# A new opening for a kernel of windowed attention followed by an expanding layer with SoLU and LayerNorm

## The chip, the cores and the metric

The kernel runs on one core of a Trainium2 chip. The metric is device time in microseconds (us) for one execution, and lower is better. The core has five engines that run side by side, each with its own queue of instructions taken in order: TensorE (PE in the profile, with its weight loads as PEld), VectorE (DVE), ScalarE (ACT), GpSimd (POOL) and SyncE (SP). In this kernel all transfers between HBM and the core's memory are issued from SP's queue. PE writes its results to PSUM, which has eight banks of 512 fp32 columns; DVE and ACT read PSUM and SBUF, POOL works on SBUF alone.

## The reference

Eight batches of eight heads, 576 positions, 64 columns a head. The first four heads attend to the last 32 positions, the other four to every fourth of the last 128. What comes out is laid side by side as 4608 tokens of 512 values, and goes through a layer with a softmax gate and a normalisation:

```python
scores = np.where(mask, (q @ k.T) / np.sqrt(64), -1e9)
attn = softmax(scores);  x = attn @ v            # 4608 tokens x 512
h = x @ w_in                                     # 512 -> 1024
solu = h * softmax(h)
ln = (solu - mean(solu)) / np.sqrt(var(solu) + 1e-6) * g_ln
out = ln @ w_out                                 # 1024 -> 512
```

The data are fp32, and so is the accuracy wanted. The two weight matrices arrive as 64-bit floats, so the kernel itself has to turn them into fp32.

## The kernel before

**Products in three passes.** A product of two fp32 matrices is made with PE's faster fp32r type: each operand is split into a high part (the value rounded to fp32r) and a low part (the rest), and hi x hi, hi x lo and lo x hi are added up in PSUM. So `w_i` and `w_o` are kept as pairs, x as `x_hi` and `x_lo`, and the normalised tile t, turned, as `th` and `tl`.

**Weights.** They come in 16 blocks of 128 x 512 values (512 KB as 64-bit words): blocks 0 to 7 make `w_in` (block b holds rows b // 2 and column half b % 2), blocks 8 to 15 `w_out`. Of each block ACT makes `low` (the lower bits) and `abs` (the magnitude), DVE does `sign`, `clamp` and `join`, which put the fp32 words together; for blocks 8 to 15 ACT multiplies with `gain` (g_ln); ACT's `hi` rounds, and `lo` subtracts the rounded from the full value. Blocks 0 to 5 make `lo` on PE: `diff` (two matmuls, with the identity and with its negative `minus`) leaves the difference in a bank of 5 to 7, and ACT copies it out. From block 6 on POOL subtracts. Raw blocks land in slots that the middle layer uses later (t0 to t3, raw4, raw5).

**Attention, in units.** A unit is two heads of one batch, 32 in all; four units make the x of one batch, 4.5 tiles of tokens. For unit n: load `q` (kt, 312 KB, and qt, 296 KB) and `v` (384 KB); `S` (80 small matmuls, L220); `mask`, `max`, `sub`, `exp`, `sum`, `inv`, `norm`, `turn` (32 x 32 blocks transposed on DVE); `V` (up to 96 small matmuls, L294); `xh` (ACT) and `xl` (DVE) write high and low part of x. In units 0 to 3 the mask is put into the bank by PE and `sub` is DVE's; from unit 4 on `mask` is DVE's and `sub` POOL's. `norm` is DVE's throughout. V writes to the front columns of banks 4 to 7.

**Tiles of 128 tokens.** For each of 36 tiles i: `ha`, `hb`, `hc`, `hd` (24 matmuls of 128 x 512 together, L328) give h in two banks; `peak` (DVE), `e` (ACT), `gate` (DVE), `mid` (centring, on ACT for the tiles in ACT_CENTRE, else on DVE), `var` (a square with its sum on ACT, then a chain of six tiny operations on POOL that end in rstd). Then t has to be turned, features to the partitions. Tiles 0 to 5 and the last do it on PE: `t` (eight transposes, L399) into banks 3 and 4, `th` (ACT) and `tl` (DVE) out of them. All others take a detour over HBM: `forth` (four DMAs, L426) writes t, `back` (one DMA, L433) fetches it with its blocks exchanged, `tr0` and `tr1` transpose inside 32 x 32 blocks on DVE (L442), `th0`, `th1` (ACT, L450) and `tl0`, `tl1` (POOL, L455) split it. `o` (24 matmuls, L464) and `out` (ACT, and a DMA) end the tile.

**What sets the order.** The order of every instruction on every engine is written out in lists of words, a word for each step and its number; each engine follows its part of the list. INIT lists the first loads, all ahead of any other work; OPENING goes from the first conversion to tile 5 and unit 9, with o0 to o4 in it. From i = FIRST = 6 on, STEP is repeated for each tile: h of tile i, attention of the units that are due, and `o` of tile k. A tile that goes over HBM needs time, so in the steady state k = i - 2; tiles 0 to 5 have k one step behind, and step 7 (NO_SECOND_STEP) has no `o` at all, since there the lag goes from one step to two. A DMA stands in SP's queue at its place in the list, and SP waits there until its data and its slot are ready.

## Time and profile before

| what | value |
|---|---|
| median of 3 runs | 537.34 us (536.75 to 538.61) |
| the profiled execution | 538.63 us, its span 536.7 us |
| mean granted clock of PE | 0.975 |
| PE busy | 500.6 us (93%) |
| DVE, ACT, POOL busy | 355.6 (66%), 240.3 (45%), 186.8 us (35%) |
| chain that ended last | PE 85%, DVE 5%, DMA 5%, ACT 2%, issue 2% |

The span goes from the first to the last instruction. "Busy" is the time in which an engine has an instruction at work. Rows of groups give line, engine, operation, output and input with their shapes, the count, then busy time in all and the mean of one in ns, then idle time before them with what released it. Rows of waits give who waits, for whom, then the total, the number of waits and the longest. Rows of a timeline give start, length, engine, line and operation. The chain of waits follows back from the last instruction what released each step. The granted clock is the share of full speed that PE was allowed.

### The profile page before, as it was taken

The page shows a single profiled execution, that of the slowest core. Times are in us where ns is not written, and L with a number is a line of the kernel's source. Part 1 is how long each engine was busy: PE and PEld are TensorE (multiplying, and loading weights), DVE is VectorE, ACT ScalarE, POOL GpSimd, SP SyncE. Part 2 cuts the span into 40 slices and gives each one's busy share as a digit, 9 for nine tenths or more (in the row PEclk, how much of TensorE's full clock was granted, in tenths as well). Part 3 has the DMA queues.
Part 4 walks back from the last instruction along what each step waited for, and adds up shares of the span by engine and source line. Part 5 has one row for each costly group of instructions (what it writes and reads, how often), then busy time and mean ns, then how long its engine had stood idle before and what let it go on. Part 6 is the DMA issues. An engine that isn't in the chain of part 4 may idle for free.

```text
span 536.7 us, 16433 instructions
## 1 busy us (share of the span) xinstructions
PE 500.6 (93%) x7186; PEld 398.8 (74%) x7186; DVE 355.6 (66%) x554; ACT 240.3 (45%) x384; POOL 186.8 (35%) x316
## 2 busy tenths in 40 slices
...
GB/s 303 400 329 153 168 0 92 94 137 52 111 164 123 251 177 176 128 145 193 175 174 177 175 175 176 153 146 196 175 176 129 100 100 100 107 127 102 100 97 59
DMA packets 42983, 82.07 MB, mean 153 GB/s; under 512 B 5024, under 2 KB 20256, under 8 KB 42912
## 3 DMA queue, kind: packets, MB, share of 16 engines
...
q14 instruction: 15, 0.12, 0.1%
...
## 4 chain that ended last, share of the span: by engine, by line
PE 85%; DVE 5%; DMA 5%; ACT 2%; issue 2%; SPq 0%; ACTq 0%; DVEq 0%
PE banks L328 36%; PE banks L464 36%; PE banks L294 6%; PE banks L220 5%; DMA raw<-w_in 2%; PE banks L399 1%; DVE t L353 1%; DMA kt<-kT 1%; DMA t<-w_in 1%; PE banks L538 1%; DVE x_lo L315 1%; DVE nmax L339 1%; ACT x_hi L312 1%; DMA raw<-mid 1%; DVE mag L521 0%
## 5 line engine op out<-in xcount | busy, mean ns | idle before, releaser
L328 PE MATMUL banks<-w_i,x_hi 128*128 128x512 f32 x576 | 186.7, 405 | 5.9 <-DVE mu L353 5.7
L464 PE MATMUL banks<-w_o,th 128*128 128x512 f32 x576 | 180.8, 395 | 0.0
L328 PEld LDWEIGHTS banks<-w_i,x_hi 128*128 128x128 f32 x576 | 108.3, 193 | 32.0 <-DVE mu L353 6.2
L464 PEld LDWEIGHTS banks<-w_o,th 128*128 128x128 f32 x576 | 106.0, 188 | 21.6
L328 PE MATMUL banks<-w_i,x_lo 128*128 128x512 f32 x288 | 114.6, 398 | 0.0
L464 PE MATMUL banks<-w_o,tl 128*128 128x512 f32 x288 | 112.3, 390 | 0.0
L339 DVE TENSOR_REDUCE nmax<-banks 128x1 f32<-128x1024 f32 x36 | 44.0, 1221 | 65.3 <-PE banks L328 65.3
L455 POOL TENSOR_TENSOR tl<-t,th 128x512 fp32r<-128x512 f32 x58 | 74.2, 1302 | 32.1 <-ACT th L450 32.1
L259 ACT ACTIVATE sm<-sm 128x640 f32<-128x640 f32 x32 | 23.6, 737 | 97.6 <-POOL sm L255 97.6
L328 PEld LDWEIGHTS banks<-w_i,x_lo 128*128 128x128 f32 x288 | 55.3, 192 | 12.3
L464 PEld LDWEIGHTS banks<-w_o,tl 128*128 128x128 f32 x288 | 54.1, 188 | 11.7
L346 ACT ACTIVATE e<-banks,nmax 128x1024 f32<-128x1024 f32 x36 | 40.2, 1116 | 50.0 <-DVE nmax L339 47.3
L374 ACT ACTIVATE e<-t 128x1024 f32<-128x1024 f32 x29 | 30.8, 1062 | 53.5 <-DVE t L369 53.5
L234 DVE TENSOR_TENSOR sm<-banks,mask_sb 128x640 f32<-128x640 f32 x28 | 23.0, 822 | 46.7 <-PE banks L220 46.4
L353 DVE CUSTOM_DVE_ANT_0 t<-banks,e 128x1024 f32<-128x1024 f32 x36 | 43.8, 1216 | 15.2 <-ACT e L346 15.1
L255 POOL TENSOR_TENSOR sm<-sm,mx 128x640 f32<-128x640 f32 x28 | 35.3, 1262 | 47.0 <-DVE mx L246 41.6
L294 PEld LDWEIGHTS banks<-pt,vt 32*64 32x64 f32 x2816 | 34.6, 134 | 19.4 <-issue 10.6
L379 POOL TENSOR_SCALAR sq<-sq 128x1 f32<-128x1 f32 x36 | 11.0, 305 | 98.5 <-ACT e L374 98.2
L294 PE MATMUL banks<-pt,vt 32*64 32x64 f32 (+3 forms) x2816 | 38.5, 230 | 7.2 <-ACT w_i L545 3.6
L220 PEld LDWEIGHTS banks<-kt,qt 64*32 64x32 f32 x2560 | 29.4, 110 | 18.1 <-issue 14.4
L220 PE MATMUL banks<-kt,qt 64*32 64x64 f32 x2560 | 35.2, 235 | 5.8 <-issue 4.6
L450 ACT CAST th<-t 128x512 fp32r<-128x512 f32 x58 | 34.5, 619 | 11.4 <-DVE t L442 11.4
...
## 6 DMA issues: line engine op xcount, KB each, us to landing
...
```

The lines of the kernel that those rows point to most:

```text
L220: nc.tensor.matmul(out=ps[WIN * c : WIN * c + WIN, h, WQ * i : WQ * i + WQ], lhsT=qt[D * h : D * h + D, q0 : q0 + WIN], rhs=kt[D * h : D * ...
L255: eng.tensor_tensor(out=st[n]["sm"], in0=st[n]["sm"], in1=wide(mx), op=ALU.subtract)
L259: nc.scalar.activation(out=sm, in_=sm, func=AF.Exp, scale=0.125)
L294: nc.tensor.matmul(out=ps_x[D * h : D * h + D, c, c0 : c0 + k1 - k0], lhsT=vt[WIN * c : WIN * c + WIN, i, D * h : D * h + D], rhs=pt[WIN * ...
L328: nc.tensor.matmul(out=ps_h(i)[:, half], lhsT=a[:, kt, xs], rhs=w_i[:, kt, half, part, :], start=(kt == 0 and k == 0), stop=(kt == KT - 1 ...
L339: nc.vector.tensor_reduce(out=nmax, in_=h, axis=AX.X, op=ALU.max, negate=True)
L346: nc.scalar.activation(out=e, in_=h, func=AF.Exp, bias=nmax, scale=1.0, accum_out=se)
L353: nc.vector.tensor_tensor_reduce(out=t, in0=h, in1=ms[i]["e"], scale=1.0, scalar=0.0, op0=ALU.mult, op1=ALU.add, accum_out=mu,)
L374: nc.scalar.activation(out=e, in_=t, func=AF.Square, accum_out=sq)
L450: nc.scalar.copy(out=ms[i]["th"][:, cut(c)], in_=turned(i)[:, cut(c)])
L455: nc.gpsimd.tensor_tensor(out=ms[i]["tl"][:, cut(c)], in0=turned(i)[:, cut(c)], in1=ms[i]["th"][:, cut(c)].bitcast(F32), op=ALU.subtract,)
L464: nc.tensor.matmul(out=ps_o(i), lhsT=a[:, f, :], rhs=w_o[:, f, part, :], start=(f == 0 and k == 0), stop=(f == FT - 1 and k == 2),)
```

## The change

- **t over HBM from tile 0.** `by_dma` holds for all tiles but the last, so `t`, `th`, `tl` by way of PE are left for tile 35 alone. The lag is two steps from the start: k = i - 2, NO_SECOND_STEP is gone. The halves of the turn are called A and B, and in the opening they may come in either order.
- **Low parts.** `diff` with its matmuls, its copies on ACT and the tile `minus` are gone; `lo` is subtracted on POOL for twelve blocks and on DVE for blocks 2, 6, 13 and 15.
- **Clamps** of all blocks but 3, 5 and 6 go from DVE to POOL.
- **Normalising** of units 0 to 7 goes from DVE to POOL.
- **Centring** of tile 3 goes to DVE, that of tile 5 to ACT.
- **Order.** INIT and OPENING become one new list for all engines, loads among it. w1 is loaded first. The list reaches o3 (before: o4), and a word of STEP that the list holds already is skipped. 
- **Places.** h of tiles 0 and 2 is in banks 0 and 1, that of all others in banks 2 and 3; `o` alternates between banks 0 and 1 from tile 0; scores use banks 2 and 3 up to unit 4 (before: up to unit 9). Raw blocks have seven slots (SLOTS), with tp. The pad in front of `th0` is 24 values rather than 32.
- **A first Exp** on a column of constants (`ready`) stands ahead of everything on ACT.

The diff, with the old list cut:

```diff
--- before.py
+++ after.py
@@ -37,63 +37,54 @@
 SIGN_BIT = -(1 << 31)
 PE_MASK = (0, 1, 2, 3)
 POOL_SUB = True
-POOL_NORM = ()
-ACT_CENTRE = (0, 1, 2, 3)
+POOL_NORM = (0, 1, 2, 3, 4, 5, 6, 7)
+POOL_CLAMP = (0, 1, 2, 4, 7, 8, 9, 10, 11, 12, 13, 14, 15)
+DVE_LOW = (2, 6, 13, 15)
+ACT_CENTRE = (0, 1, 2, 5)
 Q_BUFS, V_BUFS, T_BUFS, TH_BUFS, CONV_BUFS = 4, 4, 4, 2, 4
 REBIAS = 2.0**16
 F64_MIN = REBIAS * float(np.array(0x38000000, np.uint32).view(np.float32))
 F64_MAX = REBIAS * float(np.array(0x47EFFFFF, np.uint32).view(np.float32))
-LOW_DIFF = 'mmmmmmpppppppppp'
 FIRST = 6
-INIT = "w0 q0 ib m0 i w1 v0 q1 w2 w3 v1 m1 q2 w4 w5 v2 g q3 v3"
 OPENING = (
-    "low0 abs0 sign0 clamp0 join0 w6 S0 q4 hi0 neg0 max0 low1 sub0 abs1 "
...
+    "w1 m0 low1 ib abs1 sign1 q0 clamp1 join1 S0 hi1 w0 max0 abs0 low0 q1 sub0 sign0 exp0 w3 "
+    "low3 clamp0 join0 sum0 w2 abs2 m1 lo1 inv0 S1 abs3 max1 q2 low2 sub1 S2 norm0 w5 w4 sign3 "
+    "clamp2 w7 turn0 v0 sign2 hi0 clamp3 low4 q3 w6 join3 low5 hi3 exp1 max2 V0 sub2 q4 sign4 "
+    "sign5 abs5 exp2 lo0 sum1 w9 lo3 v1 S3 inv1 join2 low7 sum2 v3 norm1 xh0 inv2 clamp5 abs4 "
+    "max3 xl0 turn1 sub3 g norm2 hi2 v2 clamp4 S4 w8 abs7 lo2 low6 w10 q5 join4 q7 V1 clamp7 "
+    "join5 abs6 v4 sign6 hi5 clamp6 exp3 q6 join6 xh1 hi6 sign7 sum3 lo5 inv3 low10 norm3 xl1 "
+    "low9 turn2 join7 mask4 w11 sign9 V2 abs9 hi4 ha1 xh2 clamp9 low8 lo4 max4 xl2 hi7 turn3 "
+    "ha0 sub4 abs8 exp4 sign10 w13 V3 lo6 v5 abs10 join9 lo7 sum4 inv4 xh3 abs11 xl3 w12 low11 "
+    "hc0 clamp10 clamp8 hb0 gain9 w14 join10 sign8 hd0 join8 norm4 S5 peak0 mask5 clamp11 low14 "
+    "max5 hi9 gain8 hc1 hd1 lo9 v6 turn4 V4 hi8 e0 gain10 sub5 hi10 low12 gate0 sign11 join11 "
+    "ha2 xh4 low13 xl4 lo8 exp5 lo10 mid0 abs12 S6 sum5 inv5 q8 hb1 norm5 hb2 clamp12 mask6 "
+    "max6 var0 peak1 gain11 sign14 e1 sub6 abs13 turn5 q9 hc2 forth0 abs14 hd2 gate1 back0 mid1 "
+    "sign13 peak2 hi11 clamp14 sign12 V5 clamp13 xh5 var1 xl5 exp6 forth1 join12 w15 join14 "
+    "gain12 gain14 join13 sum6 lo11 S7 hi12 ha3 inv6 mask7 e2 max7 norm6 v7 hc3 hi14 gain13 "
+    "abs15 sub7 trB0 turn6 V6 low15 back1 hd3 trB1 lo14 exp7 trA0 sign15 clamp15 thA0 gate2 xh6 "
+    "lo12 hi13 thB0 q10 tlA0 hb3 xl6 mid2 sum7 lo13 join15 S8 forth2 inv7 q11 gain15 hi15 tlB0 "
+    "mask8 norm7 back2 var2 peak3 lo15 e3 turn7 gate3 mid3 o0 max8 thB1 v8 V7 xh7 xl7 q12 ha4 "
+    "var3 trA1 thA1 tlA1 out0 sub8 hc4 exp8 trB2 forth3 trA2 hd4 tlB1 S9 hb4 peak4 v9 sum8 e4 "
+    "gate4 back3 thB2 mid4 trB3 thA2 o1 ha5 inv8 tlB2 hb5 tlA2 mask9 forth4 var4 hc5 norm8 "
+    "turn8 back4 hd5 o2 V8 v10 out1 v11 max9 trA3 thB3 trA4 peak5 trB4 thA3 sub9 e5 xh8 exp9 "
+    "xl8 thA4 out2 gate5 tlA3 tlB3 mid5 forth5 back5 thB4 sum9 inv9 o3 norm9 tlB4 var5 v12 "
+    "turn9 tlA4 out3 q13 i "
 )
 STEP = (
-    "back.j tr0.k th0.k tr1.k th1.k tl0.k tl1.k ha.i hb.i S.n q.n mask.n max.n sub.n hc.i hd.i "
+    "back.j trA.k thA.k trB.k thB.k tlA.k tlB.k ha.i hb.i S.n q.n mask.n max.n sub.n hc.i hd.i "
     "V.m v.m peak.i exp.n sum.n inv.n e.i gate.i mid.i forth.i xh.m xl.m var.i norm.n turn.n "
     "o.k t.i th.i tl.i out.k"
 )
-NO_SECOND = FIRST + 1
-NO_SECOND_STEP = (
-    "back.j ha.i hb.i S.n q.n mask.n max.n sub.n tr0.j tr1.j hc.i hd.i V.m v.m peak.i exp.n "
-    "xh.m sum.n xl.m e.i inv.n gate.i th0.j th1.j tl0.j tl1.j mid.i forth.i var.i norm.n turn.n"
+LAST_STEP = (
+    "back.j trA.k thA.k trB.k thB.k tlA.k tlB.k ha.i hb.i hc.i hd.i peak.i e.i trA.j trB.j "
+    "thA.j thB.j tlA.j tlB.j gate.i mid.i var.i o.k t.i th.i tl.i out.k"
 )
-LAST_STEP = (
-    "back.j tr0.k th0.k tr1.k th1.k tl0.k tl1.k ha.i hb.i hc.i hd.i peak.i e.i tr0.j tr1.j "
-    "th0.j th1.j tl0.j tl1.j gate.i mid.i var.i o.k t.i th.i tl.i out.k"
-)
-TURN = "tr0 th0 tr1 th1 tl0 tl1".split()
-BY_DMA = ["forth", "back", *TURN]
+BY_DMA = "forth back trA thA trB thB tlA tlB".split()
 BY_PE = "t.i th.i tl.i".split()
 LAST = NTILE - 1
-MERGED = 10
-SHIFT = {"th0": 32}
+SLOTS = "t0 t1 t2 t3 raw4 raw5 tp t0 t1 t2 t3 raw4 raw5 tp t3 tp".split()
+MERGED = 5
+SHIFT = {"th0": 24}
 
 
 @with_exitstack
@@ -130,7 +121,6 @@
     )
 
     id_sb = const.tile([P, P], F32, name="id_sb")
-    minus = const.tile([P, P], F32R, name="minus")
     mask_sb = const.tile([P, 2, NS * WQ], BF16, name="mask_sb")
     g_sb = const.tile([P, FT], F32, name="g_sb")
     id_bf = const.tile([P, P], BF16, name="id_bf")
@@ -145,10 +135,10 @@
     ps_t = (banks[:, 3, :], banks[:, 4, :])
 
     def ps_h(i):
-        return banks[:, 0:2] if i <= FIRST + 1 else banks[:, 2:4]
+        return banks[:, 0:2] if i in (0, 2) else banks[:, 2:4]
 
     def ps_o(i):
-        return banks[:, 2] if i < FIRST else banks[:, i % 2]
+        return banks[:, i % 2]
 
     def ps_s(n):
         if n < MERGED:
@@ -157,6 +147,8 @@
 
     nc.vector.memset(mhalf, -0.5)
     nc.vector.memset(below, -0.5 + 2.0**-14)
+    ready = const.tile([P, 1], F32, name="ready")
+    nc.scalar.activation(out=ready, in_=mhalf, func=AF.Exp)
 
     loaded = {}
 
@@ -185,14 +177,9 @@
 
     words = {}
 
-    def raw_slot(b):
-
-        k = b % 6 if b < 12 else b - 10
-        return f"t{k}" if k < T_BUFS else f"raw{k}"
-
     def load_w(b):
 
-        words[b] = moe.tile([P, 1024], F32, name=raw_slot(b), bufs=1).bitcast(I32)
+        words[b] = moe.tile([P, 1024], F32, name=SLOTS[b], bufs=1).bitcast(I32)
         w, row, col = (w_in, P * (b // 2), 512 * (b % 2)) if b < 8 else (w_out, P * (b - 8), 0)
         nc.sync.dma_start(
             out=words[b], in_=w.bitcast(I32)[row : row + P, 2 * col : 2 * (col + 512)]
@@ -417,7 +404,7 @@
             )
 
     def by_dma(i):
-        return FIRST <= i < LAST
+        return i < LAST
 
     def move_out(i):
 
@@ -445,12 +432,12 @@
         )
 
     def high_t(i, c):
-        if c == 0:
+        if "th" not in ms[i]:
             ms[i]["th"] = part_of_t("th", i)
         nc.scalar.copy(out=ms[i]["th"][:, cut(c)], in_=turned(i)[:, cut(c)])
 
     def low_t(i, c):
-        if c == 0:
+        if "tl" not in ms[i]:
             ms[i]["tl"] = part_of_t("tl", i)
         nc.gpsimd.tensor_tensor(
             out=ms[i]["tl"][:, cut(c)], in0=turned(i)[:, cut(c)],
@@ -503,7 +490,8 @@
 
     def conv_clamp(b):
 
-        nc.vector.tensor_scalar(
+        eng = nc.gpsimd if b in POOL_CLAMP else nc.vector
+        eng.tensor_scalar(
             out=cv[b]["mag"], in0=cv[b]["mag"], scalar1=F64_MIN, scalar2=F64_MAX,
             op0=ALU.max, op1=ALU.min,
         )
@@ -528,30 +516,13 @@
         nc.scalar.activation(out=cv[b]["mag"], in_=cv[b]["mag"], func=AF.Copy, scale=gain(b))
 
     def conv_hi(b):
-        if b < 8 or LOW_DIFF[b] == "p":
-            nc.scalar.copy(out=hi(b), in_=cv[b]["mag"])
-        else:
-            nc.scalar.activation(out=hi(b), in_=cv[b]["mag"], func=AF.Copy, scale=gain(b))
-
-    def conv_diff(b):
-        ps = cv[b]["ps"] = banks[:, 5 + b % 3, :]
-        nc.tensor.matmul(out=ps, lhsT=id_sb, rhs=cv[b]["mag"], start=True, stop=False)
-        nc.tensor.matmul(out=ps, lhsT=minus, rhs=hi(b), start=False, stop=True)
+        nc.scalar.copy(out=hi(b), in_=cv[b]["mag"])
 
     def conv_lo(b):
-        lo = w_part(b)[:, 1, :]
-        kind = LOW_DIFF[b]
-        if kind == "m":
-            nc.scalar.copy(out=lo, in_=cv[b]["ps"])
-        elif kind == "p":
-            nc.gpsimd.tensor_tensor(
-                out=lo, in0=cv[b]["mag"], in1=hi(b).bitcast(F32), op=ALU.subtract
-            )
-        else:
-            nc.vector.scalar_tensor_tensor(
-                out=lo, in0=cv[b]["mag"], scalar=1.0 if b < 8 else gain(b),
-                in1=hi(b).bitcast(F32), op0=ALU.mult, op1=ALU.subtract,
-            )
+        eng = nc.vector if b in DVE_LOW else nc.gpsimd
+        eng.tensor_tensor(
+            out=w_part(b)[:, 1, :], in0=cv[b]["mag"], in1=hi(b).bitcast(F32), op=ALU.subtract
+        )
         del cv[b]
 
     one = {
@@ -560,9 +531,8 @@
         "ib": lambda _: nc.sync.dma_start(out=id_bf, in_=ident_bf),
         "g": lambda _: nc.sync.dma_start(out=g_sb, in_=g_ln),
         "m": lambda d: nc.sync.dma_start(out=mask_sb[:, d], in_=mask[:, d]),
-        "neg": lambda _: nc.scalar.mul(out=minus, in_=id_sb, mul=-1.0),
         "abs": conv_abs, "low": conv_low, "clamp": conv_clamp, "sign": conv_sign,
-        "join": conv_join, "gain": conv_gain, "hi": conv_hi, "diff": conv_diff, "lo": conv_lo,
+        "join": conv_join, "gain": conv_gain, "hi": conv_hi, "lo": conv_lo,
         "S": scores, "mask": soft_mask, "max": soft_max, "sub": soft_sub, "exp": soft_exp,
         "sum": soft_sum, "inv": soft_inv, "norm": soft_norm, "turn": turn,
         "V": attend, "xh": spread_hi, "xl": spread_lo,
@@ -570,9 +540,9 @@
         "hc": lambda i: moe_h(i, 1, (0, 1)), "hd": lambda i: moe_h(i, 1, (2, 3)),
         "peak": moe_peak, "e": moe_exp, "gate": moe_gate, "mid": moe_centre, "var": moe_var,
         "forth": move_out, "back": move_back,
-        "tr0": lambda i: turn_t(i, 0), "tr1": lambda i: turn_t(i, 1),
-        "th0": lambda i: high_t(i, 0), "th1": lambda i: high_t(i, 1),
-        "tl0": lambda i: low_t(i, 0), "tl1": lambda i: low_t(i, 1),
+        "trA": lambda i: turn_t(i, 0), "trB": lambda i: turn_t(i, 1),
+        "thA": lambda i: high_t(i, 0), "thB": lambda i: high_t(i, 1),
+        "tlA": lambda i: low_t(i, 0), "tlB": lambda i: low_t(i, 1),
         "t": moe_t, "th": moe_th, "tl": moe_tl, "o": moe_o, "out": moe_out,
     }
     fronts = {}
@@ -580,27 +550,24 @@
         for r in range(NPAIR):
             fronts[(9 * b) // 2 - NPAIR - 1 + r] = NPAIR * b + r
 
-    for word in (INIT + " " + "".join(OPENING)).split():
+    for word in OPENING.split():
         name = word.rstrip("0123456789")
         one[name](int(word[len(name) :] or 0))
+    done = set(OPENING.split())
     for i in range(FIRST, NTILE + 2):
-        of = {
-            "n": fronts.get(i), "m": fronts.get(i - 1), "i": i, "j": i - 1,
-            "k": {FIRST: FIRST - 1, FIRST + 1: None}.get(i, i - 2),
-        }
-        words_of = {NO_SECOND: NO_SECOND_STEP, LAST: LAST_STEP}.get(i, STEP)
+        of = {"n": fronts.get(i), "m": fronts.get(i - 1), "i": i, "j": i - 1, "k": i - 2}
+        words_of = {LAST: LAST_STEP}.get(i, STEP)
         for word in (words_of if i <= LAST else "o.k out.k").split():
             name, which = word.split(".")
             n = of[which]
             if n is None or which in "ijk" and n >= NTILE:
                 continue
-            if i == NO_SECOND + 1 and name in TURN and which == "k":
-                continue
             if name in BY_DMA and not by_dma(n) or word in BY_PE and by_dma(n):
                 continue
             if name in "qv":
                 n += Q_BUFS if name == "q" else V_BUFS
-            one[name](n)
+            if f"{name}{n}" not in done:
+                one[name](n)
     assert not ms and not cv
 
 
```

25 rows, old and new, of the table OPENING are left out of this document.

## The prediction

> **What bounds the kernel now.** I read the clock and the span first, then the busy time by stage, then what TensorE (PE) waits for, and only then single rows. The stages, cut where the first output product o0 begins and where the opening list ends (columns: stretch, its length, busy time of each engine, granted clock, DMA share, GB/s):
>
> ```profile
> 0.00:81.12 81.12, 51.29 (x947) 35.86 (x947) 59.13 (x100) 52.57 (x86) 19.78 (x28) 0.83 0.63 224
> 81.12:140.60 59.48, 58.74 (x995) 47.55 (x994) 41.08 (x66) 25.67 (x41) 11.75 (x27) 1.00 0.32 95
> 140.60:536.70 396.10, 390.55 (x5251) 315.42 (x5249) 255.39 (x390) 162.09 (x259) 155.25 (x262) 1.00 0.49 147
> ```
>
> From 81.12 on PE is busy 449.3 of 455.6 us at clock 1.00: PE alone sets the pace, and an engine beside it buys nothing there. Before 81.12 it is busy 51.3 us, at clock 0.83. The waits of PE over the whole span say the same:
>
> ```profile
> PE banks L212 <- DMA mask_sb<-mask: 7.4, 1, 7.4
> PE banks L328 <- DVE mu L353: 5.7, 2, 4.7
> PE banks L220 <- issue: 4.6, 2, 3.1
> PE banks L294 <- ACT w_i L545: 3.6, 2, 3.2
> PE banks L294 <- DVE pt L278: 0.7, 1, 0.7
> PE banks L294 <- DVE sm L234: 0.4, 1, 0.4
> ```
>
> The first four lie in the opening; the last two are the 1.1 us at 169, where the old list changes its lag. So the change can pay only up to the point where PE is saturated, plus PE work that it removes. What PE's work costs when nothing is late, from the chain of waits (start, length, what), and the same work early on:
>
> ```profile
> 59.66 4.61 PE banks L328 x12
> ...
> 130.31 0.97 PE banks L220 x64
> ...
> 139.97 0.87 PE banks L399 x8
> ...
> 210.54 1.01 PE banks L294 x70
> ...
> 217.21 5.44 PE banks L328 x24
> ...
> 471.40 5.44 PE banks L464 x24
> ```
>
> By 81.12 PE has done h0 to h2 (16.3), S0 to S5 (5.8) and V0 to V3 (4.0): 26 us of lasting work in 81 us. The 55 us between are the prize.
>
> **Who is late in the opening.** VectorE (DVE) is busy 59 of those 81 us, ScalarE (ACT) 53, GpSimd (POOL) 20. Two later stretches of the opening:
>
> ```profile
> 43.00:59.70 16.70, 10.11 (x262) 6.77 (x260) 15.18 (x24) 13.16 (x22) 6.22 (x5) 0.90 0.64 201
> 59.70:81.12 21.42, 16.75 (x65) 13.30 (x65) 15.88 (x25) 16.39 (x28) 13.37 (x20) 0.76 0.11 38
> ```
>
> DVE instructions overlap in the records: the sum below begins at 12.00 and the next at 12.73, though the row says 0.81. I take 0.08 off each. Then DVE works 15.18 - 24 x 0.08 = 13.3 of 16.7 us (79%) in the first stretch and 13.9 of 21.4 (65%) in the second.
>
> **The end of the sum.** The new list reaches o0 later in its own order: before it stand S0 to S8, V0 to V6 and h0 to h3. What PE has left after o0's end is the old rest less what now lies earlier or is gone: 536.70 - 81.12 = 455.6, less o0 5.4, h3 5.4, S6 to S8 2.9, V4 to V6 3.0, four of the t transposes on PE (t2 to t5) 3.5 and the gap at 169 of 1.1: 434.2. This needs PE saturated after o0. DVE then has 19 us queued for tiles 3 to 5 and units 8 and 9 in the rest of the list and POOL about 18, against 30 us of PE, so both are covered. o0 cannot end before the last low part, lo15, is there (its eighth block f=7 uses it; about 0.7 us follow). So **span = T(lo15) + 0.7 + 434.2 + stalls**, with T(lo15) to be found.
>
> **The start, to sub3.** The queue of SP in the new order puts w1, m0, ib, q0, w0, q1, w3, w2, m1, q2, w5, w4, w7 and v0 ahead of q3: by the tile shapes 6.75 MB. What the queues moved before, in slices of 2.5 us:
>
> ```profile
> GB/s 57 282 361 371 408 399 396 400 401 399 400 406 399 379 194 267 70 149 15 293 280 164 233 249 278 13 0 0 0 0 0 0 0 0 7 63 256 209 157 256
> ```
>
> Eight slices make 6.69 MB, so q3 lands at 20.2, and later by the 1.3 us by which PE's first wait (7.4) outlasts the 1.26 MB it needed (6.1). S3 takes 1.4 cold, then max3, xl0, turn1 and sub3 on DVE 2.9: 26 us, between 24 (no lateness) and 30 (one more instruction stall of 3.1, as in the wait on issue above). Loading ACT's table at the start lies under the first load; the 24 holds it.
>
> **From there to lo15.** DVE rows (mean ns, with 0.08 to come off):
>
> ```profile
> 12.00 0.81 DVE L263 TENSOR_REDUCE rs<-sm 128x10 f32<-128x640 f32 x1
> 12.73 0.68 DVE L521 SCALAR_TENSOR_TENSOR mag<-mag,low 128x512 int32<-128x512 int32 x1
> ...
> L339 DVE TENSOR_REDUCE nmax<-banks 128x1 f32<-128x1024 f32 x9 | 10.9, 1211 | 6.5 <-PE banks L328 6.5
> L353 DVE CUSTOM_DVE_ANT_0 t<-banks,e 128x1024 f32<-128x1024 f32 x9 | 10.8, 1202 | 0.5 <-ACT e L346 0.3
> L315 DVE TENSOR_TENSOR x_lo<-banks,x_hi 128x576 fp32r<-128x576 f32 x11 | 10.6, 962 | 11.7 <-ACT x_hi L312 11.7
> L278 DVE STREAM_TRANSPOSE pt<-sm 128x640 f32<-128x640 f32 x12 | 10.1, 838 | 0.1
> L414 DVE TENSOR_TENSOR tl<-banks,th 128x512 fp32r<-128x512 f32 x12 | 7.7, 682 | 3.4 <-ACT th L406 3.4
> L234 DVE TENSOR_TENSOR sm<-banks,mask_sb 128x640 f32<-128x640 f32 x9 | 7.4, 818 | 9.4 <-PE banks L220 9.4
> L246 DVE TENSOR_REDUCE mx<-sm 128x10 f32<-128x640 f32 x9 | 7.4, 817 | 0.4
> L506 DVE TENSOR_SCALAR mag<-mag 128x512 f32<-128x512 f32 x16 | 7.0, 452 | 0.9 <-ACT mag L490 0.9
> L268 DVE RECIPROCAL rs<-rs 128x10 f32<-128x10 f32 x13 | 2.8, 217 | 0.4
> L442 DVE STREAM_TRANSPOSE t<-raw 128x512 f32<-128x512 f32 x2 | 1.3, 692 | 0.1
> ```
>
> Between sub3 and lo15 the list holds 10 signs and 12 joins (22 x 0.60 = 13.2), 4 low parts (as L414, 2.4), a clamp (0.4), 4 max (3.0), 5 sums (3.7), 5 inverses (two small ones each, 1.7), 6 xl (5.3), 5 turns (3.8), 5 masks (3.7), 4 peaks (4.5), 3 gates with their reading out (3.6), 3 scalings of mu (0.3) and 3 half turns of t (1.8): **47.4 us of DVE**. The move takes 9 clamps (3.3) and 5 normalisings (3.7) off DVE here, and puts 4.2 on it with low parts and half turns. ACT has about 42 us, covered.
>
> POOL takes what was moved. Its rows:
>
> ```profile
> L255 POOL TENSOR_TENSOR sm<-sm,mx 128x640 f32<-128x640 f32 x9 | 11.4, 1262 | 27.6 <-DVE mx L246 22.2 <-DVE rs L267 5.4
> L547 POOL TENSOR_TENSOR w_i<-mag,w_i 128x512 fp32r<-128x512 f32 x2 | 2.6, 1280 | 46.9 <-ACT w_i L532 46.9
> ...
> 77.54 0.24 POOL L375 TENSOR_SCALAR se<-se 128x1 f32<-128x1 f32 x1
> 79.57 1.29 POOL L547 TENSOR_TENSOR w_o<-mag,w_o 128x512 fp32r<-128x512 f32 x1
> ```
>
> 9 low parts and 2 halves of tl at 1.28 (14.1), 5 normalisings and 4 subs at 1.26 (11.4), 3 variance chains at 2.03 (6.1: 77.54 to 79.57). A clamp on POOL is in no row: it lies between DVE's 0.45 and POOL's two-input 1.28; I take the middle, 0.87, so 9 make 7.8 (4 to 11.5). **POOL: 39 us**, under DVE's 47 only if the two run side by side. They do not always:
>
> ```profile
> 60.32 1.30 DVE L513 SCALAR_TENSOR_TENSOR low<-t,low 128x512 int32<-128x512 int32 x1
> 61.54 2.37 DVE L513 SCALAR_TENSOR_TENSOR low<-raw,low 128x512 int32<-128x512 int32 x2
> ...
> 59.77 2.99 POOL L547 TENSOR_TENSOR w_o<-mag,w_o 128x512 fp32r<-128x512 f32 x2
> ```
>
> While POOL subtracted low parts, three signs took 3.7 us instead of 2.1, and POOL's two took 3.0 instead of 2.6: operations with two SBUF inputs delay each other. The Trainium skill has this as a rule (SBUF — State Buffer, Who interferes with whom): a Vector instruction with two SBUF inputs, or in a two-port mode, and a GpSimd instruction exclude one another for a whole instruction. By that rule signs, joins, DVE's low parts and its clamp (16.0) add to POOL's 39.3 and the stretch takes 55.3 at least, so lo15 at 81; without it 47.4, lo15 at 73; the trace agrees with it in these rows.
>
> My value does not need the rule: at the 79% that DVE reached from 43.00 to 59.70, 47.4 us last 60, so **T(lo15) = 26 + 60 = 86**. Bounds: DVE never idle, 73; the 65% of the stretch in which POOL was busy most, 73 us, so 99. I stay by the first, because the second stretch holds two waits of DVE for PE, at a halved clock (59.66 against 217.21):
>
> ```profile
> DVE nmax L339 <- PE banks L328: 4.7, 2, 2.8
> ```
>
> Without them it is 13.9 of 16.7 us, 83%, and POOL was busy 62% of it, as it will be now (39 of 60). The new list has four tiles and nine units at hand where the old had two tiles and six.
>
> **Stalls.** h4 writes the banks that gate3 still reads, and gate3 stands just behind lo15: 1 us. A cold start of o0: 12 cold matmuls cost 1.9 more, I take 1 (0 to 2). Behind forth and back on SP wait w15, v7, q10 and later loads; back0 must wait for forth0 to land.
>
> ```profile
> 152.35 1.78 SPq L426 DMA_DIRECT2D mid<-t  x4
> ...
> 156.09 0.34 SPq L433 DMA_DIRECT2D raw<-mid  x1
> ```
>
> From the first forth to the issue of back 3.7 us pass with SP blocked. Tile 0's centring falls near 55, tile 1's near 63, so w15 is issued near 66 and its conversion is listed behind V6 near 73: covered by some 3 us, and each us over is one of T(lo15). Six detours more (6 MB) run where DMA is at 0.11 to 0.32. The diffs on PE lay before 81 and only shorten the opening, as their banks no longer hold V0 back (3.6 above). Addresses move by the tile taken away: costed at nothing, at most 3 us either way, 25 V's at 0.12 more or less.
>
> **Sum:** 86 + 0.7 + 434.2 + 2 = 522.9 of span. The profiled execution took 538.63 at a span of 536.7 (1.9 around it), and the median of the runs is 1.3 below it: 523.5 as a run.
>
> **Rivals.**
> (A) DVE and POOL dovetail: DVE works 86% to 100% of the stretch, lo15 at 73 to 81, so 511 to 518.5. For it: 9 clamps and 5 normalisings less, and clock and banks freed. Against: the rows at 60.
> (B) The pace stays that of 59.70 to 81.12 (65%): lo15 at 99, run 536.5: no change. PE then starves as long as before, only behind a longer list.
> (C) Slower: the second-input conflict between sub3 and o0. Every POOL operation holds DVE's next sign or join, and each join waits for a clamp queued on POOL behind a low part or a normalising of 1.3. Wholly in series 47.4 + 39.3 = 87, lo15 at 113, run 550. It decides from lo15 at 101.5, when 28 of POOL's 39 us are paid by DVE. For it: the three signs paid 1.6 of POOL's 3.0. Against: 31 of DVE's 47 us are reductions, turns and reads of PSUM, whose means show no such stretching.
> (D) PE isn't saturated behind o0, since the detour makes tiles 0 to 3 late: each late half stalls PE by some 2 us, at most 8 over four tiles: 531. Against: o1 lies 13 us of PE behind o0.
>
> **Chances.** Forecast (518.5 to 530) 0.52; A 0.20; D and the stretch from 530 to 535.5 0.11; B 0.06; C 0.11. This kernel's measurement tells about 0.3% (1.6 us) from no change. Faster: 0.83, same 0.06, slower 0.11. The likeliest one's own range is 518 to 530; to leave out no more than 2 in 10, 511 to 537.
>
> **What would show it.** Right: o0 (L464's first row) begins at 80 to 86 and ends within 1 us of L547's last low part; DVE between 26 and 86 at about 80%; no PE wait over 1 us afterwards; no L399 before the last tile. Signs and joins beside POOL should average over 0.75. Wrong: lo15 above 99, a PE wait on tl or th behind o0, a clamp on POOL above 1.3, or a steady step other than before.

## The result and the profile after

The changed kernel took 524.06 us (median of 4 runs, 523.53 to 524.79), the kernel before 537.05 us beside it (535.85 to 538.61). The ratio is 0.976, with a 95% interval of 0.973 to 0.979. The profiled execution took 523.99 us at a span of 522.2 us, with a mean clock of PE of 0.993 (before 0.975). So 14.5 us of span are gone, and the forecast of 523.5 us was right. Of its two large terms, one was too small and the other too large, and that the two errors cancel to within a microsecond is luck.

The stages come first, in the window view of the changed kernel (stretch, its length, busy time of PE, PEld, DVE, ACT and POOL, granted clock, DMA share, GB/s). They are cut at the end of sub3, at the end of the last low part (lo15) and at the end of o0:

```profile
0.00:31.20 31.20, 10.30 (x424) 7.20 (x424) 21.97 (x35) 15.90 (x25) 16.05 (x15) 1.00 0.95 357
31.20:89.10 57.90, 43.38 (x1033) 33.96 (x1034) 54.57 (x79) 42.53 (x66) 49.73 (x41) 0.94 0.55 179
89.10:92.66 3.56, 3.56 (x24) 2.70 (x25) 2.34 (x6) 1.21 (x3) 2.98 (x8) 1.00 0.95 322
92.66:522.20 429.54, 425.81 (x5649) 345.04 (x5648) 274.90 (x421) 179.26 (x285) 174.41 (x290) 1.00 0.50 153
```

Up to 31.2 the DMA engines are busy 95%. From there to 89.1 DVE is busy 54.6 of 57.9 us and POOL 49.7, both more than foreseen. From 92.66 on PE has 3.7 us without work in 430, where the kernel before had 6.3 in the 455.6 after its own cut at 81.12.

The same two stretches that the prediction read of the kernel before show, in the changed one, how DVE came to be occupied:

```profile
43.00:59.70 16.70, 14.44 (x300) 10.61 (x298) 16.26 (x20) 12.41 (x20) 15.35 (x10) 1.00 0.42 133
59.70:81.12 21.42, 14.55 (x373) 11.76 (x374) 18.86 (x31) 15.88 (x26) 17.75 (x22) 0.92 0.55 172
```

DVE is busy 97% and 88% of them, where it was 91% and 74%. POOL is at 92% and 83%, where it was 37% and 62%.

What PE waited for, over the whole span of the changed kernel (who waits, for whom; total, times, longest):

```profile
PE banks L281 <- DVE pt L265: 9.6, 3, 5.0
PE banks L199 <- DVE sm L239: 6.2, 3, 4.1
PE banks L207 <- DMA t<-w_out: 5.6, 1, 5.6
...
PE banks L451 <- POOL tl L442: 0.4, 1, 0.4
```

All of these lie before o0 ends; from 92.66 on this view has no row at all. The two largest are PE's waits for what DVE makes out of scores. The four that led before (mask, mu, instructions, w_i) are gone or smaller.

The chain of waits around o0 (start, length, what):

```profile
81.37 2.25 POOL mag L494
83.62 1.26 POOL w_o L523
84.88 2.46 POOL tl L442
...
87.38 5.28 PE banks L451 x22
```

What ends last ahead of o0's third matmul is POOL: a clamp of 2.25 us, a low part and the first half of tl. After that the chain is PE alone.

Where the gain is complete can be read from the starts of the outputs. First the kernel before, then the changed one (chain of waits again, `o` of tiles 6 and 7 in each):

```profile
171.27 5.68 PE banks L464 x24
184.73 5.69 PE banks L464 x24
```

```profile
158.10 5.67 PE banks L451 x24
171.53 5.68 PE banks L451 x24
```

At tile 6 the changed kernel is 13.2 us ahead of the old one, of the 14.5 in the end. The step shown lasts 13.4 to 13.5 us in both kernels. So nearly all of the change pays in its first 158 us; of the other 1.3 us, some 0.4 come near 447 of the old kernel, where a V took 1.41 us instead of 1.01, and 0.6 ahead of its last transposes.

**The books.** The old span is 81.12 + 455.58, the new one 92.66 + 429.54. The rest begins 11.5 us later and is 26.0 us shorter. Of these 26.0, work that still has to be done but now lies ahead of the cut makes 16.7 (o0 5.4, h3 5.4, S6 to S8 2.9, V4 to V6 3.0, all priced in the prediction). So the opening gained 16.7 - 11.5 = 5.2 us and the rest 26.0 - 16.7 = 9.3 us: together 14.5.

### The profile page after: what moved, and what is told of

It is laid out like the page before. It is cut to its first block, busy times and chain, and to the rows that moved or that the text cites. A ratio compares the mean times of both kernels' runs of the same rounds, so it can differ in the third digit from the quotient of the medians.

```text
span 522.2 us, 16362 instructions
## 1 busy us (share of the span) xinstructions
PE 483.1 (93%) x7120; PEld 388.9 (74%) x7120; DVE 353.8 (68%) x537; ACT 238.9 (46%) x378; POOL 243.2 (47%) x351
## 4 chain that ended last, share of the span: by engine, by line
PE 83%; DVE 6%; POOL 5%; DMA 4%; issue 1%; ACT 1%; SPq 0%; ACTq 0%; POOLq 0%; DVEq 0%
PE banks L451 39%; PE banks L315 34%; PE banks L281 5%; PE banks L207 4%; POOL mag L494 2%; DVE mag L509 2%; DMA raw<-w_in 1%; DMA t<-w_in 1%; DMA qt<-qT 1%; DVE low L501 1%; POOL w_o L523 1%; DVE rs L250 1%; DVE pt L265 1%; POOL sm L242 1%; POOL sm L260 0%
## 5 line engine op out<-in xcount | busy, mean ns | idle before, releaser
L315 PE MATMUL banks<-w_i,x_hi 128*128 128x512 f32 x576 | 184.4, 402 | 0.0
L442 POOL TENSOR_TENSOR tl<-t,th 128x512 fp32r<-128x512 f32 x70 | 91.1, 1321 | 41.2 <-ACT th L437 41.1
L315 PEld LDWEIGHTS banks<-w_i,x_lo 128*128 128x128 f32 x288 | 55.0, 191 | 13.2 <-DVE x_lo L302 0.9
L361 ACT ACTIVATE e<-t 128x1024 f32<-128x1024 f32 x35 | 37.2, 1062 | 53.6 <-DVE t L356 53.6
L340 DVE CUSTOM_DVE_ANT_0 t<-banks,e 128x1024 f32<-128x1024 f32 x36 | 44.0, 1222 | 16.7 <-ACT e L333 16.6
L437 ACT CAST th<-t 128x512 fp32r<-128x512 f32 x70 | 41.8, 619 | 16.5 <-DVE t L429 16.0
L242 POOL TENSOR_TENSOR sm<-sm,mx 128x640 f32<-128x640 f32 x28 | 35.9, 1280 | 25.7 <-DVE mx L233 25.7
L362 POOL TENSOR_SCALAR se<-se 128x1 f32<-128x1 f32 x36 | 8.7, 242 | 81.8 <-ACT e L333 81.3
```

Of the source, the lines that this page charges most:

```text
L242: eng.tensor_tensor(out=st[n]["sm"], in0=st[n]["sm"], in1=wide(mx), op=ALU.subtract)
L315: nc.tensor.matmul(out=ps_h(i)[:, half], lhsT=a[:, kt, xs], rhs=w_i[:, kt, half, part, :], start=(kt == 0 and k == 0), stop=(kt == KT - 1 ...
L340: nc.vector.tensor_tensor_reduce(out=t, in0=h, in1=ms[i]["e"], scale=1.0, scalar=0.0, op0=ALU.mult, op1=ALU.add, accum_out=mu,)
L361: nc.scalar.activation(out=e, in_=t, func=AF.Square, accum_out=sq)
L437: nc.scalar.copy(out=ms[i]["th"][:, cut(c)], in_=turned(i)[:, cut(c)])
L442: nc.gpsimd.tensor_tensor(out=ms[i]["tl"][:, cut(c)], in0=turned(i)[:, cut(c)], in1=ms[i]["th"][:, cut(c)].bitcast(F32), op=ALU.subtract,)
```

## The experiments

The theories that the expectations set against each other were these. DVE's work sets the pace of the opening, and what leaves DVE helps. Against it: POOL, or the way in which POOL holds up DVE, sets it, so that undoing the moves helps. A third says that loads and PE's supply of instructions set the beginning, and a faster DVE or POOL gains nothing there. For the parts alone: the moves without the new order make the old kernel slower, and PE work put back behind o0 costs its full length. Ratios are to the kernel before, measured beside each experiment; its medians there were 537.3 to 539.4 us, against 537.05 beside the changed kernel. So a difference of 1 or 2 us between an experiment and the changed kernel is not clear of the noise.

**Clamps back on DVE.**

```diff
-POOL_CLAMP = (0, 1, 2, 4, 7, 8, 9, 10, 11, 12, 13, 14, 15)
+POOL_CLAMP = ()
```

> The changed kernel with all 16 clamps on DVE again. Theory 1 (the prediction's: DVE sets the pace of the opening, and every us taken off it pays): DVE gets 13 x 0.34 us more, 9 of them in the stretch up to the last low part, at its pace of about 80% some 4 us, so about 528 us. Theory 2 (POOL sets the pace near the first output product, since its clamp takes 1.92 us where DVE's takes 0.34, and joins wait for it): 17 us leave POOL in that stretch and the first join comes 1.5 us earlier, so 515 to 521 us.

It took 524.4 us, 0.975 of the kernel before (0.970 to 0.979): the same as the changed kernel. The window from 31.2 to 89.1 and the group of joins, in this kernel:

```profile
31.20:89.10 57.90, 44.17 (x1036) 34.74 (x1037) 55.72 (x88) 41.34 (x64) 30.54 (x33) 0.94 0.53 174
```

```profile
L509 DVE SCALAR_TENSOR_TENSOR mag<-mag,low 128x512 int32<-128x512 int32 x16 | 12.7, 802 | 0.2
```

POOL fell from 49.7 to 30.5 us, but DVE rose by 1.1 only, although it had nine instructions more in this stretch (88 against 79): the joins became shorter. The same group in the kernel before, then in the changed kernel with the signs of most blocks and the clamps on POOL (group view):

```profile
L521 DVE SCALAR_TENSOR_TENSOR mag<-mag,low 128x512 int32<-128x512 int32 x16 | 11.7, 743 | 0.0
```

```profile
L509 DVE SCALAR_TENSOR_TENSOR mag<-mag,low 128x512 int32<-128x512 int32 x16 | 15.8, 992 | 4.3 <-POOL mag L494 4.1
L501 DVE SCALAR_TENSOR_TENSOR low<-t,low 128x512 int32<-128x512 int32 x9 | 6.5, 719 | 5.0 <-ACT low L487 5.0
...
L494 POOL TENSOR_SCALAR mag<-mag 128x512 f32<-128x512 f32 x13 | 27.0, 2081 | 9.9 <-ACT mag L477 9.7
```

A join costs 0.99 us beside the clamps on POOL and 0.80 without them, and the joins wait 4.1 us less for clamps in all. Clamps take DVE 7.4 us in all here against 2.3 for the three it keeps in the changed kernel, 5.1 more. The signs (12.7 us in the changed kernel) take 2.0 more. Against this the joins take 3.1 less and wait 4.1 less (2.6 of it ahead of sub3), and DVE's own low parts take 1.2 less. That adds up to about nothing. So both theories missed: the move takes work from DVE, and DVE gives about as much back in longer operations and in waits for clamps. One thing clouds the balance: PE stops for 3.1 us in S3 here, which it doesn't in the changed kernel (the experiment without clamps below shows such a stop). sub3 ends at 31.6 instead of 31.2, and what the time would be without the stop isn't shown.

**Normalising back on DVE, then both back.**

```diff
-POOL_NORM = (0, 1, 2, 3, 4, 5, 6, 7)
+POOL_NORM = ()
```

> The changed kernel with the normalising of units 0 to 7 on DVE again, clamps on POOL. Theory 1 (DVE sets the pace): 5 x 0.74 us more DVE in the stretch, so about 529 us. Theory 2 (POOL sets it): 8 x 1.26 us leave POOL and turns no longer wait for a normalising queued behind a clamp of 1.9 us, so 520 to 524 us.

525.1 us, 0.975 (0.971 to 0.979): again no difference, and again neither theory (529, and 520 to 524 us) was met.

> The changed kernel with clamps and normalising both on DVE. Theory 1 (DVE sets the pace): 7 us more DVE in the stretch, 533 us. Theory 2 (POOL sets it): POOL falls to about half of its load, DVE is the pacer at 47.4 + 6.8 us; at 90% that is 60 us and hardly another time than the 58 us measured, so 519 to 525 us.

Both edits together took 526.58 us, 0.977 (0.974 to 0.981). That is 2.5 us above the changed kernel by the medians and 0.9 by the ratios, and the intervals overlap. The window of this kernel:

```profile
31.20:89.10 57.90, 39.83 (x1002) 31.36 (x1006) 57.31 (x86) 38.89 (x61) 26.55 (x30) 0.94 0.49 166
```

DVE is busy 99%, and o0 begins at 89.50 instead of 86.27. Both moves together are worth 1 to 2.5 us, by the spans of the profiled executions 4.1, out of 14.5. Of the two theories (533 us if DVE's work sets the pace, 519 to 525 if POOL's does) neither was met.

**A clamp of one operation.** A clamp is a max and a min in one instruction.

```diff
-            out=cv[b]["mag"], in0=cv[b]["mag"], scalar1=F64_MIN, scalar2=F64_MAX,
-            op0=ALU.max, op1=ALU.min,
+            out=cv[b]["mag"], in0=cv[b]["mag"], scalar1=F64_MIN, scalar2=None, op0=ALU.max,
```

> The changed kernel whose clamp has one operation (the maximum) in place of two; the minimum is left out, which these data do not need. It measures the price of the clamp on POOL by itself. If its 1.92 us come from the two operations, it falls to about 1.3 us or under, and the time falls by 1 to 4 us; if they come from the 512 values or from the instruction alone, it stays at 1.9 us, and the time too.

522.14 us, 0.969 (0.964 to 0.974). The first undisturbed clamp on POOL in the changed kernel, with the subtraction behind it, and then in this one (timeline: start, length):

```profile
10.75 1.92 POOL L494 TENSOR_SCALAR mag<-mag 128x512 f32<-128x512 f32 x1 [2.78 <-ACT mag L477]
12.63 1.27 POOL L523 TENSOR_TENSOR w_i<-mag,w_i 128x512 fp32r<-128x512 f32 x1
```

```profile
9.70 1.49 POOL L494 TENSOR_SCALAR mag<-mag 128x512 f32<-128x512 f32 x1 [2.25 <-ACT mag L477]
```

The clamp falls to neither of the values expected (1.3 or under, or still 1.9): the min costs POOL 0.43 us, and even with max alone the clamp is longer than a subtraction of two tensors. The rows settle the price of a clamp on POOL: 1.92 us, 4.3 times DVE's average of 0.45 in the kernel before.

**The old kernel with low parts as in the new one.** The old order stays; `diff`, its copies and `minus` go.

```diff
-LOW_DIFF = 'mmmmmmpppppppppp'
+LOW_DIFF = 'ppvpppvppppppppp'
```

> The kernel before with its low parts alone changed: no differences on PE, blocks 2 and 6 subtract on DVE, all others on POOL; its own order, clamps and normalising stay on DVE. Theory 3 (after the runs that undo the moves: the moves to POOL pay nothing, the gain is in the freed banks 5 to 7 and in the new order): the 3.6 us of V0 behind the copied differences and the 2.5 us of the differences behind x_lo go, 530 to 533 us. Theory 4 (the order and the detour alone bring the gain, the low parts nothing): 535 to 538 us.

536.15 us, 0.998 (0.995 to 1.001): no difference, as the theory had it that the low parts alone bring nothing (535 to 538 us). PE's waits in this kernel:

```profile
PE banks L294 <- DVE pt L278: 7.3, 3, 4.7
...
PE banks L328 <- POOL w_i L547: 2.4, 1, 2.4
```

V's wait of 3.6 us for the banks of `diff` is gone. A wait for DVE's turned probabilities and one for POOL's low part stand in its place.

**The old kernel with both moves.** Only POOL_CLAMP and POOL_NORM, as in the new kernel, in the old order.

```diff
-POOL_NORM = ()
+POOL_NORM = (0, 1, 2, 3, 4, 5, 6, 7)
+POOL_CLAMP = (0, 1, 2, 4, 7, 8, 9, 10, 11, 12, 13, 14, 15)
```

> The kernel before in its own order with the same 13 clamps and the normalising of units 0 to 7 on POOL. Theory 1 (the prediction's: DVE's relief pays by itself): 13 x 0.34 + 8 x 0.74 us less DVE, 530 to 533 us. Theory 5 (the move pays only where the order puts other work between a clamp and its join; here each join follows its clamp closely and waits for 1.9 us on POOL): 540 to 552 us.

540.85 us, 1.006 (1.004 to 1.009): slower. Of the two theories, the one that has DVE's relief pay by itself (530 to 533 us) fell; the one that has joins wait for clamps (540 to 552) held, at its lower end: the joins took 14.7 us (11.7 before) and waited 7.7 us for POOL's clamps, where they had waited for none. The opening of this kernel, to set beside the prediction's first row:

```profile
0.00:81.12 81.12, 48.77 (x934) 33.51 (x935) 55.66 (x80) 52.18 (x84) 47.42 (x38) 0.83 0.63 224
```

POOL took on 27.6 us and DVE lost 3.5.

**No clamp at all.**

```diff
-        eng = nc.gpsimd if b in POOL_CLAMP else nc.vector
-        eng.tensor_scalar(
...
+        return
```

> The changed kernel without any clamp (the clamp is left out; these data do not need it). It bounds what the 13 clamps of 1.9 us on POOL cost, waits and all. Theory 2 (they are on the way to the first output product): 25 us of POOL and 1 us of DVE go, 514 to 518 us. Theory 3 (the pace is set by the loads and by the chain of DVE): 519 to 522 us.

522.91 us, 0.971 (0.968 to 0.975). Taking every clamp away buys 1 to 2 us, from two runs, and the intervals overlap. PE's longest wait in this kernel behind its first load, inside S3 (timeline):

```profile
24.24 0.43 PE L207 MATMUL banks<-kt,qt 64*32 64x64 f32 x5
28.81 1.36 PE L207 MATMUL banks<-kt,qt 64*32 64x64 f32 x75 [4.14 <-issue]
```

PE stops for 4.1 us in S3 with nothing shown that it waits for ("issue"). sub3 ends at 33.3 instead of 31.2, so what the clamps left free is at least in part spent there. The same stop, 3.1 to 3.6 us, stands in the kernels with clamps on DVE, with both back, with the clamp of one operation, and in the last one below; the changed kernel doesn't have it. This fits the third theory for the beginning: whoever is faster meets the next limit.

**The detour undone.** Tiles 0 to 4 are turned on PE again, in the new order, into banks 0 and 1: the words of the detour leave the list, `t`, `th` and `tl` of these tiles come in, and the identity is loaded earlier. Tile 0's transposes are written over h of tile 2 before gate2 has read it, so tile 2 is computed from other values; the amount of work is the same.

```diff
-    ps_t = (banks[:, 3, :], banks[:, 4, :])
+    ps_t0 = (banks[:, 3, :], banks[:, 4, :])
...
+        return (banks[:, 0, :], banks[:, 1, :]) if i < 5 else ps_t0
...
-        return i < LAST
+        return 5 <= i < LAST
```

> The changed kernel and its order, but tiles 0 to 4 are turned on PE again (eight transposes each, high part on ACT, low part on DVE) and use no detour; tile 5 and later as they are. Theory 6 (the detour pays by the PE work it takes off: five times 0.87 us and a change of shape of 0.25 us each): 528 to 530 us. Theory 7 (the two low halves queued on POOL hold the first output product, so without them it begins some 3 us earlier): 524 to 526 us.

544.86 us, 1.011 (1.008 to 1.015). Its second longest wait of PE:

```profile
PE banks L455 <- DVE tl L405: 8.6, 2, 6.1
```

I had put `tl` of tile 2 right ahead of o1 and `tl` of tile 4 right ahead of o3. These two write one of the banks that `tl` reads, and PE stood 6.1 and 2.6 us, of the 21 by which this span is longer than the changed kernel's. Both theories (528 to 530 and 524 to 526 us) missed. So the run shows what sharing these banks costs in a list that doesn't allow for it, and not what the detour is worth. The worth of the detour in the opening stays open; a list in which these transposes have banks of their own was not tried.

**No signs.** The signs of the weights are left out, 16 operations of DVE with two inputs from SBUF, and nothing is given to POOL for them.

```diff
+        return
```

(as the first line of the function that makes them)

> The changed kernel without the sign step of the conversion (the signs are left out, so all weights come out positive). It takes 16 x 0.61 us off DVE, 10 of them between sub3 and the last low part, and touches POOL only by the conflict of two SBUF inputs. Theory 1 (DVE sets the pace of the opening): 6 us less DVE in that stretch, o0 some 6 us earlier, 514 to 518 us. Theory 8 (neither DVE nor POOL alone: the chains from load to turn and the banks do): 521 to 524 us.

517.48 us, 0.961 (0.959 to 0.964): the largest gain of all runs, 6.0 us of span less than the changed kernel. The window of this kernel:

```profile
31.20:89.10 57.90, 49.99 (x1031) 39.55 (x1021) 49.64 (x70) 44.16 (x69) 48.08 (x49) 0.91 0.65 214
```

PE is busy 6.6 us more in the stretch, and o0 begins at 80.33 instead of 86.27. The signs were 12.7 us of DVE (6.5 + 3.8 + 2.4), and about half reached the end. So DVE's own work does set the pace of the opening, as the theory of 514 to 518 us had it, though not alone: in the same stretch DVE now waits for others, most of all for ACT (waits of DVE):

```profile
DVE x_lo L302 <- ACT x_hi L299: 4.5, 6, 1.3
```

**Dummy transposes.** Eight transposes of 128 x 128 on PE ahead of each of o0 to o4, whose results nobody reads; the identity that they use is loaded earlier.

```diff
+        if i < 5:
+            for f in range(8):
+                c = GQ + P * (f % 2)
+                nc.tensor.transpose(
+                    out=banks[:, 4 + f // 2 % 2, c : c + P], in_=id_sb, identity=id_sb
+                )
```

> The changed kernel with eight transposes of the identity on PE ahead of each of o0 to o4, into columns of banks 4 and 5 that nobody reads: the PE work that the detour saves, put back without anything else. Theory 6 (the detour pays by the PE work it takes off, since PE is saturated from o0 on): 5 x 0.87 = 4.4 us more, 528.5 us. If it hides in waits of the opening, 524 to 526 us.

536.24 us; the span is 533.6, that is 11.4 more than the changed kernel's. First the wait that they made, then two of their five rows (waits, timeline):

```profile
PE banks L452 <- DVE x_lo L302: 6.0, 2, 4.5
```

```profile
111.67 1.03 PE L452 MATMUL banks<-id_sb 128*128 128x128 f32 x8
...
139.73 1.97 PE L452 MATMUL banks<-id_sb 128*128 128x128 f32 x8 [4.51 <-DVE x_lo L302]
```

The time is 7.7 us above the 528.5 that was expected. The dummies share banks 4 and 5 with V's results, and ahead of o3 and o4 they wait 6.0 us until DVE has read these. After the stop of 4.5 us PE is slow (a granted clock of 0.50 from 139.7 to 143): the eight take 1.97 us, and o4 runs from 141.35 to 148.22, 6.9 us for the 5.6 of the changed kernel. What the work itself costs shows where PE doesn't wait, ahead of o1 and o2: what stands behind o0, o1 and o2 (V7, h5, V8) begins 0.49 us early, 0.41 late and 1.34 late against the changed kernel, so the sets ahead of o1 and o2 cost 0.90 and 0.93 us, near the 0.87 of the prediction's row. Ahead of o0 the dummies cost nothing, for o0 then finds its low half of t ready. So where PE is saturated, work that is put back costs its whole length; the rest of the 11.4 us is the wait for the banks and the slow stretch behind it.

**S beside V in the steady step.** A step has twelve matmuls of h, S, twelve matmuls of h, V, o. Here S stands directly ahead of V, and the words of ACT, DVE and POOL follow.

```diff
-    "back.j trA.k thA.k trB.k thB.k tlA.k tlB.k ha.i hb.i S.n q.n mask.n max.n sub.n hc.i hd.i "
-    "V.m v.m peak.i exp.n sum.n inv.n e.i gate.i mid.i forth.i xh.m xl.m var.i norm.n turn.n "
+    "back.j trA.k thA.k trB.k thB.k tlA.k tlB.k ha.i hb.i hc.i hd.i S.n q.n V.m v.m "
+    "peak.i e.i mask.n max.n sub.n gate.i mid.i forth.i xh.m xl.m exp.n sum.n inv.n var.i norm.n turn.n "
```

> The changed kernel with a steady step in which the scores of unit n stand right ahead of V of the unit before, behind hd, and the steps of the softmax behind peak and e. It does the same work with one change of matmul shape less on PE for each of 22 units. Theory 9 (a change of shape costs PE 0.25 us, as h behind S took 2.96 where it takes 2.72 else): 22 x 0.24 = 5.3 us less, 518.5 us. If the chain from scores to turn gets late in the step, or a change from S to V costs as much, 524 us or more.

528.84 us, 0.983 (0.980 to 0.987): slower than the changed kernel. One undisturbed step of it (chain of waits), then what PE waited for from 92 on, then one of these waits (timeline):

```profile
238.85 5.68 PE banks L451 x24
244.54 5.44 PE banks L315 x24
249.97 0.97 PE banks L207 x64
250.94 1.13 PE banks L281 x73
252.07 5.68 PE banks L451 x24
```

```profile
PE banks L281 <- issue: 5.1, 3, 2.0
PE banks L451 <- issue: 1.5, 2, 1.1
```

```profile
186.43 0.33 PE L281 MATMUL banks<-pt,vt 32*64 32x16 f32 x15 [2.00 <-issue]
186.69 0.99 PE L451 MATMUL banks<-w_o,th 128*128 128x512 f32 x2
...
191.14 0.62 PE L451 MATMUL banks<-w_o,th 128*128 128x512 f32 x2
```

A step takes 13.22 us from o to o, against 13.46 in the changed kernel. One change to small matmuls and back less saves about 0.25 us. Over the 22 steps that have both S and V that is 5.5 us, but the span grew by 7.7 (522.2 to 529.9), so 13 were lost. In the waits 6.6 of them are found, all on "issue": S and V are now some 170 small matmuls with as many weight loads in two microseconds, and PE stops near the end of such a stretch or in the `o` right behind it. After the stop of 2.00 us a pair of matmuls takes 0.99 instead of 0.62, for about 4 us. The three longest stops (1.3, 1.8 and 2.0 us) cost some 1.6 us more each in that way, for `o` took 7.3 us instead of 5.7. The other 1.8 or so of the 13 I have not assigned.

**Work placed by what each engine does best.** Clamps on DVE, all low parts on POOL, normalising of units 0 to 9 on POOL.

```diff
-POOL_NORM = (0, 1, 2, 3, 4, 5, 6, 7)
-POOL_CLAMP = (0, 1, 2, 4, 7, 8, 9, 10, 11, 12, 13, 14, 15)
-DVE_LOW = (2, 6, 13, 15)
+POOL_NORM = (0, 1, 2, 3, 4, 5, 6, 7, 8, 9)
+POOL_CLAMP = ()
+DVE_LOW = ()
```

> The changed kernel with the work shared between DVE and POOL by what each asks for it: a clamp takes 1.92 us on POOL for 0.34 on DVE, a low part 1.28 for 0.60, a normalising 1.26 for 0.74, so all clamps go to DVE, all low parts and the normalising of units 0 to 9 to POOL. DVE gets 4.4 us and gives 2.4 + 1.5, POOL gives 25 and gets 7.6. Theory 1 with the price of the conflict (DVE sets the pace, and POOL's long clamps stretch it): 519 to 522 us, the fastest here. Theory 8 (DVE's sum alone decides, and it has hardly changed): 523 to 525 us. If the low parts of the last blocks queue too late on POOL: 525 to 528 us.

526.52 us, 0.978 (0.975 to 0.981): not faster than the changed kernel, and inside what was expected if the last low parts queue too late on POOL. The trace shows that queue: lo15, now on POOL, ends at 92.7 instead of 89.1, and o0 stands 1.0 us for it. The stop in S3 is there too, with 3.3 us. No complete version that I ran beats the changed kernel clear of the noise.

## Why the prediction was right, step by step

**The sum.** It was 522.9 us of span, and 522.2 came. Its terms were off by more, and offset each other. What it had right is the frame: the last low part falls near the predicted time, DVE is the busiest engine up to there, and PE is saturated behind o0. The closeness of the sum is luck:

| term | predicted | measured | difference |
|---|---|---|---|
| start to sub3 | 26 | 31.2 | +5.2 |
| sub3 to lo15 | 60 | 57.9 | -2.1 |
| lo15 to the end of o0 | 0.7 | 3.56 | +2.9 |
| rest behind o0, with stalls | 436.2 | 429.5 | -6.7 |

**The start, mis-sized by 5.2.** The rows (timeline of the changed kernel, PE then DVE):

```profile
21.27 1.69 PE L281 MATMUL banks<-pt,vt 32*64 32x32 f32 x96 [2.02 <-DMA vt<-vw]
...
23.91 1.77 PE L207 MATMUL banks<-kt,qt 64*32 64x64 f32 x80
```

```profile
24.71 0.81 DVE L250 TENSOR_REDUCE rs<-sm 128x10 f32<-128x640 f32 x1
...
28.11 0.82 DVE L233 TENSOR_REDUCE mx<-banks 128x10 f32<-128x640 f32 x1
...
30.38 0.82 DVE L239 TENSOR_TENSOR sm<-banks,mx 128x640 f32<-128x640 f32 x1
```

S3 began at 23.9, and the sum had it at 21.5 (20.2 and the 1.3 of PE's first wait). q3 landed near 22.6 (issued at 14.44, 8.2 us on the way), and S3 stood behind V0 in PE's queue, which had waited 2.0 us for its own load, and then behind sub2's reading of the bank (0.3) and the mask's two matmuls. It took 1.77 for 1.4. It ended at 25.7, but max3 began at 28.1: sum1, join2, sum2 and clamp5 (with two inverses) stood ahead of it in DVE's queue. The step from max3 to the end of sub3 took 3.1, near the 2.9 of the working. So the working counted loads by bytes and left out what is queued on PE ahead of S3 and on DVE ahead of max3. The bound of 30 was broken too.

**From sub3 to lo15, right in size by luck.** 57.9 us against 60. The prediction took 0.08 us off each instruction for overlap and read 79%. But the busy time of a window already merges overlapping records: the groups of the changed kernel add up to 58.9 us in the stretch where the window says 54.6. So the overlap was taken off twice. The old pace was 91%, not 79%, and the new one is 94%. In the same step the durations were too short. The 12 joins in the stretch took 12.0 us for 8.3 at an undisturbed 0.69, the 10 signs 7.95 for 6.9, and DVE's 4 low parts 4.0 for 2.7: 6 us that DVE's operations with two SBUF inputs take longer beside POOL. Work that was undervalued and a pace that was undervalued gave nearly the right product: 47.4 of 57.9 us is 82%.

**POOL, mis-sized.** A clamp was priced at 0.87, at most 1.28, and took 1.92 alone and 2.08 on average. This is one of the things that the prediction said would make it wrong ("a clamp on POOL above 1.3"). The time held all the same, since lo15 came at 89.1 and not above 99. The experiment with clamps back on DVE shows why so little hung on that price: within the noise, and with a stop of PE that the changed kernel lacks, the moved clamps are worth nothing net.

**lo15 was not the gate.** The sum let o0 end 0.7 us after lo15; it ended 3.56 after. PE and POOL around it in the changed kernel:

```profile
79.76 1.08 PE L281 MATMUL banks<-pt,vt 32*64 32x64 f32 x80 [3.61 <-DVE pt L265]
80.77 0.98 PE L315 MATMUL banks<-w_i,x_hi 128*128 128x512 f32 x2
...
86.27 0.73 PE L451 MATMUL banks<-w_o,th 128*128 128x512 f32 x2
87.38 0.50 PE L451 MATMUL banks<-w_o,tl 128*128 128x512 f32 x1 [0.38 <-POOL tl L442]
```

V6 waited 3.6 us for turn6, which began at 78.86, when the normalising on POOL had ended. The 12 matmuls of h3 behind it began at a lower clock (0.65 granted from 79.76 to 84.1, and 0.98 us for a pair that takes 0.62 else) and ended at 85.3, and o0 began at 86.27. Its low half came from POOL 0.4 us later still. At 89.1 o0 had nine of its 24 matmuls done, and the other fifteen followed without a stop. The late step here is a queue on POOL, of the kind that C described, at a small price.

**The rest, mis-sized by 6.7 in the good direction.** The two stalls of 2 us did not come, and PE's waits behind the cut vanished altogether. Of the old 2.4 us of them, the prediction had counted 1.1; the others, 1.3, are these rows of the kernel before (from 81.12 on):

```profile
PE banks L294 <- issue: 0.9, 3, 0.6
...
PE banks L399 <- DVE tp L369: 0.4, 1, 0.4
```

The other 3.4 were not foreseen. The steady-step experiment gives a cause for a part: a change between small and large matmuls and back costs about 0.25 us, and six S's and V's fewer stand behind the cut, which makes some 1.4 by this price. The transposes that went add hardly anything to that, since eight of them cost 0.90 to 0.93 where 0.87 was counted. The 1.4 was worked out from that run and not measured by itself, and the other 2 or so stay open.

**The rivals.** A (dovetail) needed lo15 by 81; even without the signs it came at 83.8. B (the pace of the stretch from 59.70 on) fell: DVE is busy 88% there, where it was 74%. C (POOL holds DVE) was real at 6 us and far from its 28. In the old order the moves alone show C's waits deciding the sign: 7.7 us of joins waiting for clamps, and 0.6% slower. D fell: no wait of PE on a half of t behind o0.

**What was said to show it.** Kept: no wait of PE behind o0 (the view has no row), transposes on PE for the last tile alone, signs and joins beside POOL above 0.75 (0.79 and 0.99 on average). Missed: o0's beginning at 86.27 (80 to 86), its end 3.56 us after lo15 (1), DVE at 94% (80%).

**What the gain is made of.** Low parts alone are worth nothing in the old order, moves alone cost 0.6% there, and in the new order both moves undone cost 1 to 4 us. So most of the 14.5 us, 10 or more, lies in what remains. By the books above 9.3 come behind o0: the four transposes gone (3.5, a price that the dummies bear out), the old waits gone (2.4), and 3.4 of which 1.4 are explained. The other 5.2 come in the opening, from the new order with the detour in it and from whatever the moves add. How these 5.2 divide was not shown; the run that should have said so was ruled by its own waits.
